# The second batch of a fused linear-attention and channel-mix kernel: loads and attention by halves of heads, later weights in another order

## Chip, cores and metric

The kernel runs on one core of a Trainium2 chip. The metric is the device time of one execution in microseconds (us); lower is better. Inputs are float32 in HBM (the chip's main memory), the output is float32, and the matrix work is done in bf16 with float32 sums in PSUM.

## The reference

Two stages, one after the other, on 8 batches of 576 tokens with 8 heads of 64 (so 512 channels):

```python
kv  = einsum('bhsd,bhse->bhde', k, v)              # 64 x 64 for each head: no softmax
out = einsum('bhsd,bhde->bhse', q, kv)
out = out / sqrt(mean(out * out, -1) + 1e-6) * g_norm       # by head
x   = out.transpose(0, 2, 1, 3).reshape(B, S, 512)
x_prev = x shifted by one token (zeros first)
xk = mu_k * x + (1 - mu_k) * x_prev                # likewise xr with mu_r
kk = maximum(xk @ w_k, 0)                          # 512 -> 1024
v  = (kk * kk) @ w_v                               # 1024 -> 512
y  = sigmoid(xr @ w_r) * v                         # 512 -> 512
```

## The kernel before

Nothing is scheduled by a compiler. One list of words, `ORDER`, is walked from its first word to its last, and each word emits its instructions. An engine executes its own instructions in the order in which they were emitted, so the list is the schedule of every engine. The list has eight strings, one about for each batch. A word reads like this: `Kp.0.1.2'=4` is the operation `Kp` with arguments 0, 1, 2; the mark `'` puts its evacuation (the copy out of PSUM) on VectorE instead of ScalarE; the digits after `=` name the PSUM banks (0 to 7) that it takes. A bank is given back by the operation that reads it last, so a word that takes a bank waits for that reader.

The work of one batch and the words for it:

- `ld` (line 188): loads k, v or q of a batch with a cast to bf16, issued on the GpSimd queue (POOL). The tiles for batches 1 to 7 have one buffer for each of k, v and q, so the load for the next batch waits for the last read of the present one. Batch 1 is loaded before the list begins, as are the weights, in the order w_k (two column halves), k, v, q, w_r, w_v (two row halves).
- `kv`, `kvo`: the 64 x 64 products of all heads and their copies; `qt`, `qto`: transposes of q for a half of the heads (M is 0 or 1) and their copies; `u`: q times kv, in three parts (token tiles 2 and 3; tiles 0 and 1; the odd first 64 tokens); `sq`, `red`, `nw`: squares on ScalarE, their sums on VectorE, and eight small VectorE steps for 1/rms by Newton's method; `mul`: times 1/rms; `x`, `x0` and `xo`, `x0o`: transposes back to channels by tokens, into `xT`.
- `dif`, `sc`, `fu`, `add`, `wrap`: differences of neighbouring tokens and the mixes `xk` and `xr`.
- `K`, `Kp` (line 485): xk times w_k with a Relu; `ks`, `ksp`: the squares, into `sqk`; `V` (line 521): a tile of 128 tokens of the product with w_v, in two parts of four matmuls; `R` (line 511): the product with w_r and the sigmoid; `fin` (line 534): their product and the store.

Batch 0 has its own path with words that end in c (`kvc`, `qtc`, `uc`, `sqc`, `msc`, `rsc`, `mcc`): its rms is a matmul with a matrix of 1/64 (`msc`) and ScalarE's Abs_reciprocal_sqrt (`rsc`). `Kp.0.0.n` are the eight pieces of batch 0 for tokens 256 to 575 ("high"), `Kp.0.1.n` the four for tokens 0 to 255 ("low"). `tab` loads ScalarE's table set with the sigmoid; the set with Abs_reciprocal_sqrt is loaded at the start. `wm.n` emits n matmuls of zeros whose result nobody reads. The last tile of the last batch is done by `L.0` and `L.1`, in two halves of the columns.

The prediction follows TensorE through the first of the eight strings, up to `Kp.1.0.0`, the first Relu product of batch 1, which opens the second.

Of the kernel before, what the change touches and what calls it, by code (L numbers as in the profile page):

```python
# [9 lines left out]
FP32 = mybir.dt.float32  # L10
# [9 lines left out]
    wm.2=1 cast.1' wm.4=2 cast.0 wm.1=3 kvc.0.2=45 kvco.0' kvco.1' qtc.0.2=67 qtco.0 qtco.1' uc.1=0 sqc.1 uc.0=1  # L20
    sqc.0 qtc.2.2=23 qtco.2' qtco.3' cols=4 msc.1=5 rsc.1 msc.0=7 rsc.0 mcc.0 mcc.1 difh.0.0.256.576 wm.2=6
    sc.0.0.1.256.576' kvc.2.1=2 kvco.2 uc.4=3 kvc.3.1=5 kvco.3 sc.0.0.0.256.576' uc.2=4 sqc.2 uc.3=6 sqc.3
    uc.5=7 sqc.5 msc.2=2 rsc.2 add.0.0.0.256.576 mcc.2 wm.4=1 msc.3=0 rsc.3 mcc.3 difh.0.1.256.576
    fu.0.0.2.256.576 sqc.4 msc.4=5 rsc.4 fu.0.0.3.256.576 Kp.0.0.0'=1 wrap.0 msc.5=2 rsc.5 mcc.5 mcc.4
    dif.0.0.256 fu.0.0.0.0.256 fu.0.0.1.0.256 sc.0.1.0' fu.0.0.3.0.256 fu.0.0.2.0.256 tab Kp.0.0.1=0 Kp.0.0.2=4
    Kp.0.0.3=6 Kp.0.0.4'=5 Kp.0.0.5=1 sc.0.1.1 sc.0.1.2 add.0.1.0 ksp.0.0.0.4 sc.0.1.3 add.0.1.1 Kp.0.0.6=2
    Kp.0.0.7'=7 Kp.0.1.0=3 Kp.0.1.1=0 Kp.0.1.2'=4 ksp.0.1.0.4 Kp.0.1.3=6 kv.1=15 kvo.1.0' ld.0.2 qt.1.0=23
    qto.1.0.0' qt.1.1=70 qto.1.1.0 qto.1.0.1' kvo.1.1 qto.1.1.1' u.1.0=41 sq.1.0.0 sq.1.0.1 red.1.5.9 u.1.2=6
    sq.1.2.0 u.1.1=23 sq.1.1.0 sq.1.1.1 red.1.0.5 nw.1.0.1 nw.1.1.2 nw.1.2.3 R.0.0=7 R.0.1=5 nw.1.3.4 R.0.2=0
    R.0.3=7 V.0.2.0=5 V.0.0.0=0 ksp.0.1.4.8 V.0.3.0=7 V.0.0.1 nw.1.4.5 nw.1.5.6 nw.1.6.7 ksp.0.0.4.8 nw.1.7.8  # L30
    mul.1.0.0 mul.1.0.1 x.1.2.2=41 xo.1.2.2.0 mul.1.1.0 V.0.2.1 xo.1.2.2.1 mul.1.1.1 x.1.0.2=23 mul.1.2.0
    x0.1=64 xo.1.0.2.1 x0o.1.1 fin.0.0 V.0.3.1 dif.1.384.576 xo.1.0.2.0' V.0.1.0=0 x0o.1.0' sc.1.0.2.384.576'
    sc.1.0.3.384.576' V.0.1.1 sc.1.0.0.384.576 sc.1.0.1.384.576 adda.1.0.384.576 wrap.1 dif.1.0.384
    sc.1.0.0.0.384' sc.1.0.1.0.384' sc.1.0.3.0.384 ld.1.2
    """,
    """
    Kp.1.0.0=1 Kp.1.0.1=3 Kp.1.0.2=2 sc.1.0.2.0.384' kv.2=46 kvo.2.0 kvo.2.1 ld.2.2 fin.0.1 add.1.0.1.0.384
    qt.2.1=10 sc.1.1.1' qto.2.1.0 add.1.0.0.0.384 ld.0.3 qt.2.0=32 qto.2.0.0' sc.1.1.3 sc.1.1.0' qto.2.0.1
    Kp.1.0.3=4 Kp.1.1.0=6 Kp.1.1.1=1 Kp.1.1.2=3 qto.2.1.1' u.2.0=02 add.1.1.0 u.2.2=4 sq.2.2.0 u.2.1=61 sq.2.1.1
    sq.2.1.0 fin.0.2 fin.0.3 sc.1.1.2' add.1.1.1 sq.2.0.1 sq.2.0.0 Kp.1.1.3'=5 R.1.4=7 ksp.1.1.0.2 red.2.0.5  # L40
    red.2.5.9 nw.2.0.1 nw.2.1.2 nw.2.2.3 ld.1.3 R.1.5=3 R.1.6=5 R.1.7=7 R.1.8=3 nw.2.3.4 nw.2.4.5 nw.2.5.6
    nw.2.6.7 nw.2.7.8 mul.2.1.0 Kp.1.1.4=5 mul.2.0.0 Kp.1.1.5=7 ksp.1.1.2.4' Kp.1.1.6=3 Kp.1.1.7=5 V.1.4.0=6
    mul.2.1.1 mul.2.2.0 ksp.1.1.4.6 ksp.1.1.6.8 kv.3=07 mul.2.0.1 x.2.0.4=31 xo.2.0.4.1' wrap.2 xo.2.0.4.0
# [73 lines left out]
def kernel(  # L117
# [13 lines left out]
    nc = tc.nc  # L131
# [121 lines left out]
    def half(i):  # L253
        return slice(64 * i, 64 * i + 64)
# [288 lines left out]
    for name in "kvq":  # L543
        load(name, 1)
# [99 lines left out]
```

## Time and profile before

| what | value |
|---|---|
| median of 3 runs | 204.22 us (204.13 to 204.47) |
| the profiled execution | 203.88 us, of which 202.1 us are the profile's span |
| TensorE (PE) busy | 192.2 us, 95% |
| VectorE (DVE) / ScalarE (ACT) busy | 161.8 us, 80% / 140.3 us, 69% |
| last matmul ends | 197.78 us |
| granted TensorE clock, mean | 0.995 |

The span is cut into stretches; "busy" is the time with at least one instruction on the engine, and an engine's idle time is put down to what released it. Matmuls are pipelined, so a row for 36 small matmuls can be longer than the time that passes until the next group starts.

### The profile page before, as it was taken

How to read it: one execution, taken by the hardware profiler on the slowest of the kernel's cores; microseconds unless marked ns; L12 is line 12 of the kernel's file. 1: busy time of each engine (PE TensorE's matmuls, PEld its weight loads, DVE VectorE, ACT ScalarE, POOL GpSimd, SP SyncE). 2: the span in 40 equal slices, each digit the busy share in tenths (PEclk: the TensorE clock that was granted, in tenths of full speed). 3: DMA queues.
4: the chain of work that ended last, by engine and by line, in shares of the span. 5: the costliest groups of instructions: out<-in, count | busy, mean ns of one | idle time of the engine just before them, and what ended most of it. 6: DMA issues, size and time to landing. Idle time of an engine off the chain costs nothing.

```text
span 202.1 us, 6329 instructions
## 1 busy us (share of the span) xinstructions
PE 192.2 (95%) x2684; PEld 116.4 (58%) x2684; DVE 161.8 (80%) x350; ACT 140.3 (69%) x273; POOL 24.1 (12%) x40
## 2 busy tenths in 40 slices
PE   7877889999999999999999999999999999999991
PEld 2534764485555568466565766576575455755450
DVE  1478859999979799998999999998898979974241
ACT  3476989579887888718897898977857474542420
POOL 7750040030021002202010004000000000000000
PEclk9999999999999999999999999999999999999998
DMA  6999999969959940998955604990001502226074
GB/s 208 217 206 207 208 209 205 209 143 175 246 83 218 224 130 0 157 224 208 203 79 104 159 2 63 206 284 15 5 0 29 131 0 55 67 48 145 3 190 123
DMA packets 21360, 27.22 MB, mean 135 GB/s; under 512 B 1740, under 2 KB 16340, under 8 KB 21332
## 3 DMA queue, kind: packets, MB, share of 16 engines
q0 software_dynamic: 14848, 16.19, 49.6%
q1 hardware_dynamic: 6164, 10.23, 18.4%
q10 hardware_dynamic: 320, 0.39, 0.7%
q8 instruction: 21, 0.34, 0.7%
q14 instruction: 7, 0.06, 0.1%
HBM read 33.56 MB, written 9.44 MB: 213 GB/s over the span
## 4 chain that ended last, share of the span: by engine, by line
PE 92%; DVE 4%; ACT 1%; issue 0%
PE ps_v L521 30%; PE ps_km L485 29%; PE ps_r L511 16%; PE ps_warm L245 4%; PE ps_u L307 3%; PE ps_qt L285 2%; PE ps_kv L271 2%; PE ps_x L363 2%; DVE xk L467 1%; DVE xT L440 1%; PE ps_v L529 1%; DVE qT L203 1%; PE ps_kv L400 1%; DVE dx L455 1%; ACT rs L436 1%; PE ps_ms L432 1%
## 5 line engine op out<-in xcount | busy, mean ns | idle before, releaser
L485 PE MATMUL ps_km<-xk,wk_sb 128*128 128x288 bf16 (+4 forms) x512 | 67.8, 286 | 1.5 <-DVE xk L467 1.5
L521 PE MATMUL ps_v<-wv_sb,sqk 128*128 128x512 bf16 x280 | 64.9, 379 | 0.0
L485 PEld LDWEIGHTS <-wk_sb 128*128 128x128 bf16 x512 | 49.2, 98 | 19.9 <-issue 1.7
L489 ACT ACTIVATE rt<-ps_km 128x288 bf16<-128x288 f32 (+3 forms) x87 | 36.0, 430 | 22.9 <-PE ps_km L485 20.2
L521 PEld LDWEIGHTS <-sqk 128*128 128x128 bf16 x280 | 26.7, 98 | 29.4
L511 PE MATMUL ps_r<-wr_sb,xr 128*128 128x512 bf16 x144 | 33.9, 379 | 0.0
L534 DVE TENSOR_TENSOR out_sb<-ps_v,sig 128x512 f32<-128x512 f32 (+1 forms) x37 | 23.9, 669 | 11.1 <-ACT sig L514 8.6
L514 ACT ACTIVATE sig<-ps_r 128x512 bf16<-128x512 f32 x36 | 21.3, 603 | 13.0 <-PE ps_r L511 9.3
L495 ACT ACTIVATE sqk<-rt 128x576 bf16<-128x576 bf16 (+4 forms) x32 | 24.2, 781 | 0.1
L461 ACT ACTIVATE m<-dx,cols 128x576 bf16<-128x576 bf16 (+2 forms) x27 | 18.7, 741 | 5.5 <-DVE dx L455 5.5
L511 PEld LDWEIGHTS <-xr 128*128 128x128 bf16 x144 | 13.7, 98 | 15.0 <-DVE xr L478 0.3
L316 DVE TENSOR_REDUCE ss<-sq 128x16 f32<-128x1024 bf16 (+1 forms) x14 | 18.7, 1347 | 3.1 <-ACT sq L312 2.9
L348 DVE TENSOR_TENSOR y<-ps_u,rs 128x512 bf16<-128x512 f32 (+1 forms) x35 | 20.0, 628 | 0.3
L312 ACT ACTIVATE sq<-ps_u 128x512 bf16<-128x512 f32 (+1 forms) x35 | 16.6, 562 | 2.7 <-PE ps_u L307 2.5
L491 DVE TENSOR_SCALAR rt<-ps_km 128x288 bf16<-128x288 f32 (+3 forms) x33 | 14.6, 463 | 1.7 <-PE ps_km L485 1.5
L188 POOL DMA_DIRECT2D in_k<-in_k_dram x7 | 5.2, 743 | 85.6 <-PE ps_kv L271 74.2
L201 ACT COPY qT<-ps_qt 128x576 bf16<-128x576 bf16 x20 | 12.4, 636 | 4.0 <-PE ps_qt L409 2.7
L478 DVE TENSOR_TENSOR xr<-m,xT 128x1152 bf16<-128x1152 bf16 x16 | 12.0, 752 | 1.8 <-ACT m L461 1.5
L463 DVE TENSOR_SCALAR m<-dx,cols 128x576 bf16<-128x576 bf16 (+3 forms) x39 | 12.6, 356 | 0.2
L478 DVE TENSOR_TENSOR xk<-m,xT 128x1152 bf16<-128x1152 bf16 (+2 forms) x16 | 11.1, 698 | 1.4 <-ACT m L461 1.2
L455 DVE TENSOR_TENSOR dx<-xT 128x2304 bf16<-128x2304 bf16 (+4 forms) x11 | 11.3, 1031 | 0.7
L497 DVE TENSOR_TENSOR sqk<-rt 128x576 bf16<-128x576 bf16 (+1 forms) x25 | 11.1, 453 | 0.7 <-ACT rt L489 0.7
(63 smaller groups left out, 143.5 us busy)
## 6 DMA issues: line engine op xcount, KB each, us to landing
out_dram<-out_sb SPq DMA_DIRECT2D x68, 128.0 KB, 3.4
in_k<-in_k_dram POOLq DMA_DIRECT2D x7, 576.0 KB, 6.4
in_v<-in_v_dram POOLq DMA_DIRECT2D x7, 576.0 KB, 10.1
in_q<-in_q_dram POOLq DMA_DIRECT2D x7, 576.0 KB, 12.8
wk_sb<-in_moe_w_k_dram POOLq DMA_DIRECT2D x2, 512.0 KB, 10.3
wv_sb<-in_moe_w_v_dram POOLq DMA_DIRECT2D x2, 512.0 KB, 20.8
sqk<-in_k_dram SPq DMA_DIRECT2D x1, 576.0 KB, 3.8
q<-in_q_dram POOLq DMA_DIRECT2D x2, 288.0 KB, 6.6
```

The lines of the kernel that those rows point to most:

```text
L312: ACT.activation(out=sq[:, rg(t0, n, i) if n else slice(0, 1)], in_=held["u", a, part, i][1], func=AF.Square)
L316: DVE.tensor_reduce(out=ss[:, g0:g1], in_=sq[:, g0:g1], op=ALU.add, axis=AX.X)
L348: DVE.tensor_mul(out=y[:, g], in0=give(("u", a, part, i)), in1=rs[:, g].unsqueeze(3).to_broadcast([128, max(n, 1), NHP, HD]))
L461: eng.activation(out=out_, in_=in_, func=AF.Copy, scale=mu)
L478: DVE.tensor_add(out=dst, in0=m[:, hs, c0:c1], in1=x[:, hs, c0:c1])
L485: nc.tensor.matmul(ps[:, n, :], wk_sb[:, cc, 128 * fc:128 * fc + 128], at[b]["xk"][:, cc, c0:c1], start=(cc == 0), stop=(cc == NHP - 1))
L489: eng.activation(out=dst, in_=ps, func=AF.Relu)
L495: eng.activation(out=sqk[:, fcs, o:o + n], in_=src, func=AF.Square)
L511: nc.tensor.matmul(ps, xr[:, cc, 128 * t:128 * t + 128], wr_sb[:, cc, :], start=(cc == 0), stop=(cc == NHP - 1))
L514: ACT.activation(out=sig[b, t], in_=give("r"), func=AF.Sigmoid)
L521: nc.tensor.matmul(ps, sqk[:, fc, 128 * t:128 * t + 128], wv_sb[:, fc, :], start=(fc == 0), stop=(fc == NFC - 1))
L534: DVE.tensor_mul(out=o, in0=give(key), in1=sig[b, t][:, c])
```

## The change

The second batch (batch 1) gets operations for a half of its heads, M = 0 or 1: `kvh`, `kvho`, `uh`, `sqh`, `redh`, `rsh`, `mulh`, `x0h`, `x0ho`, `xh`, `xho`. They do what the words without h do, on two of the four head pairs. Its 1/rms is `rsh`, Abs_reciprocal_sqrt on ScalarE, in place of the eight Newton steps. Its loads are six halves, and w_v is loaded as one half and two quarters: the order after w_k is k, q, v of the first half, w_v's first half, k, q, v of the second half, w_v's two last quarters, w_r. `Vq` is `V` with two matmuls for each part; batch 0's four tiles in the first string use it. `ORDER` is written anew in all its eight strings; the first is shown, and from the last its end.

```diff
@@ ORDER, first string @@
-    wm.2=1 cast.1' wm.4=2 cast.0 wm.1=3 kvc.0.2=45 kvco.0' kvco.1' qtc.0.2=67 qtco.0 qtco.1' uc.1=0 sqc.1 uc.0=1
-    sqc.0 qtc.2.2=23 qtco.2' qtco.3' cols=4 msc.1=5 rsc.1 msc.0=7 rsc.0 mcc.0 mcc.1 difh.0.0.256.576 wm.2=6
-    sc.0.0.1.256.576' kvc.2.1=2 kvco.2 uc.4=3 kvc.3.1=5 kvco.3 sc.0.0.0.256.576' uc.2=4 sqc.2 uc.3=6 sqc.3
-    uc.5=7 sqc.5 msc.2=2 rsc.2 add.0.0.0.256.576 mcc.2 wm.4=1 msc.3=0 rsc.3 mcc.3 difh.0.1.256.576
-    fu.0.0.2.256.576 sqc.4 msc.4=5 rsc.4 fu.0.0.3.256.576 Kp.0.0.0'=1 wrap.0 msc.5=2 rsc.5 mcc.5 mcc.4
...
+    wm.4=1 wm.4=2 cast.1' cast.0 kvc.0.2=34 qtc.0.2=56 qtco.0' kvco.0' uc.0=7 qtco.1 kvco.1 uc.1=0 sqc.0 msc.0=1
+    qtc.2.2=25 qtco.2' sqc.1 msc.1=3 rsc.0 cols=6 mcc.0 qtco.3' kvc.2.1=4 rsc.1 kvco.2 uc.2=1 mcc.1
+    difh.0.0.256.576 sc.0.0.1.256.576' kvc.3.1=2 kvco.3 sqc.2 uc.5=6 uc.3=3 msc.2=4 sqc.3 msc.3=7 rsc.2
+    sc.0.0.0.256.576' rsc.3 sqc.5 add.0.0.0.256.576 uc.4=5 msc.5=2 sqc.4 msc.4=0 rsc.4 wm.2=4 rsc.5 mcc.2 mcc.3
+    wm.2=7 difh.0.1.256.576 wrap.0 fu.0.0.2.256.576 fu.0.0.3.256.576 mcc.4 Kp.0.0.0=1 Kp.0.0.1=3 mcc.5
+    dif.0.0.256 sc.0.1.1 sc.0.1.3 fu.0.0.0.0.256 fu.0.0.2.0.256 Kp.0.0.2=4 Kp.0.0.3'=0 Kp.0.0.4=7 sc.0.1.0
+    fu.0.0.1.0.256 fu.0.0.3.0.256 Kp.0.0.5=2 Kp.0.0.6'=5 Kp.0.0.7'=1 Kp.0.1.0=6 ksp.0.0.0.4 qt.1.0=30 qto.1.0.0'
+    sc.0.1.2' qto.1.0.1' kvh.0=47 kvho.0.0' kvho.0.1 Kp.0.1.1=5 add.0.1.1 uh.0.0=12 uh.1.0=63 sqh.1.0.0
+    sqh.1.1.0 uh.2.0=0 sqh.2.0.0 ksp.0.0.4.8' ksp.0.1.0.4' redh.0.5.0 sqh.0.1.0 sqh.0.0.0 Kp.0.1.2=4 Kp.0.1.3=7
+    Vq.0.3.0=5 Vq.0.3.1 rsh.0.5.0 redh.5.9.0 mulh.2.0.0 Vq.0.2.0=4 Vq.0.2.1 rsh.5.9.0 x0h.0=70 ksp.0.1.4.8
+    mulh.0.0.0 mulh.0.1.0 xh.2.2.0=12 mulh.1.0.0 xho.2.2.0.0 mulh.1.1.0 x0ho.0.1' x0ho.0.0 qt.1.1=63 qto.1.1.0
+    xh.0.2.0=10 xho.2.2.0.1' kvh.1=72 qto.1.1.1' kvho.1.1 kvho.1.0' uh.1.1=36 xho.0.2.0.0 uh.0.1=72 xho.0.2.0.1'
+    uh.2.1=0 sqh.1.1.1 sqh.2.0.1 sqh.1.0.1 redh.0.5.1 Vq.0.1.0=1 Vq.0.1.1 Vq.0.1.2 Vq.0.2.2 sqh.0.1.1 sqh.0.0.1
+    redh.5.9.1 rsh.0.5.1 mulh.1.1.1 rsh.5.9.1 Vq.0.3.2 Vq.0.3.3 mulh.2.0.1 Vq.0.0.0=6 Vq.0.0.1 mulh.0.0.1 ld.0.2
+    Vq.0.0.2 mulh.1.0.1 xh.0.2.1=07 mulh.0.1.1 xh.2.2.1=32 Vq.0.2.3 add.0.1.0 xho.2.2.1.1' tab Vq.0.1.3
+    xho.0.2.1.1' xho.2.2.1.0 dif.1.384.576 sc.1.0.0.384.576' sc.1.0.2.384.576 ld.1.2 sc.1.0.3.384.576' x0h.1=23
+    wrap.1 x0ho.1.1' x0ho.1.0 xho.0.2.1.0 R.0.0=7 R.0.1=2 dif.1.0.384 sc.1.0.1.0.384' sc.1.0.3.0.384
+    sc.1.0.2.0.384' R.0.2=3 sc.1.0.1.384.576' adda.1.0.384.576 R.0.3=0 sc.1.1.0 Vq.0.0.3 fin.0.0 sc.1.0.0.0.384
+    sc.1.1.1
...
@@ ORDER, end of the last string @@
-    fin.6.3 R.7.6=5 fin.7.4 R.7.7=4 V.7.6.1 fin.7.5 V.7.7.0=3 V.7.7.1 fin.7.6 fin.7.7 R.7.8=1 L.0=7 L.1=0
+    V.7.5.0=6 V.7.5.1 R.7.5=7 R.7.6=3 R.7.7=4 fin.6.3 fin.7.4 fin.7.5 fin.7.6 V.7.7.0=0 V.7.7.1 R.7.8=2 fin.7.7
+    L.0=5 L.1=7 wm.1=6
@@ loads ahead of the list @@
-    load_w(wk_sb, moe_w_k, cols_=2)
-    for name in "kvq":
-        load(name, 1)
-    load_w(wr_sb, moe_w_r)
-    load_w(wv_sb, moe_w_v, rows_=2)
+    for what in "wk.0.2 wk.1.2 k.0.2 q.0.2 v.0.2 wv.0.2 k.1.2 q.1.2 v.1.2 wv.2.4 wv.3.4 wr.0.1".split():
+        name, i, n = what.split(".")
+        (load_x if name in dram else load_w)(name, int(i), int(n))
     warm(12)
@@ new functions (some of them) @@
+    def load_x(name, i, n):
+        if i == 0:
+            x_in[name, 1] = inp.tile([128, NHP, GX], BF16, tag=f"in_{name}", name=f"in_{name}")
+        ms = slice(NHP // n * i, NHP // n * (i + 1))
+        nc.gpsimd.dma_start(out=x_in[name, 1][:, ms], in_=by_token(dram[name], 1)[:, ms])
+    def square_h(part, i, M):
+        sq, (t0, n) = mine(1, "sq", [128, NRG, NHP, HD], BF16), TILES[part]
+        ACT.activation(out=sq[:, rg(t0, n, i) if n else slice(0, 1), pair(M)], in_=held["uh", part, M, i][1],
+                       func=AF.Square)
+    def reduce_h(g0, g1, M):
+        sq, ss = at[1]["sq"], mine(1, "ss", [128, NRG, NHP], FP32)
+        DVE.tensor_reduce(out=ss[:, g0:g1, pair(M)], in_=sq[:, g0:g1, pair(M)], op=ALU.add, axis=AX.X)
+    def root_h(g0, g1, M):
+        ss, y = at[1]["ss"], mine(1, "rs", [128, NRG, NHP], FP32)
+        ACT.activation(out=y[:, g0:g1, pair(M)], in_=ss[:, g0:g1, pair(M)], func=AF.Abs_reciprocal_sqrt,
+                       scale=1.0 / HD, bias=eps)
+    def mult_h(part, i, M):
+        y, rs, (t0, n) = mine(1, "y", [128, NRG, NHP, HD], BF16), at[1]["rs"], TILES[part]
+        g = rg(t0, n, i) if n else slice(0, 1)
+        DVE.tensor_mul(out=y[:, g, pair(M)], in0=give(("uh", part, M, i)),
+                       in1=rs[:, g, pair(M)].unsqueeze(3).to_broadcast([128, max(n, 1), 2, HD]))
...
-    def vv(b, t, part):
+    def vv(b, t, part, n=4):
...
-        for fc in range(4 * part, 4 * part + 4):
+        for fc in range(n * part, n * part + n):
```

## The prediction, as it was written before the run

> **What bounds the kernel now.** I read the page's slices first: where is TensorE not full?
>
> ```profile
> PE   7877889999999999999999999999999999999991
> ACT  3476989579887888718897898977857474542420
> DMA  6999999969959940998955604990001502226074
> ```
>
> TensorE (PE) is full from the seventh slice (30 us) to the last; what can be won lies before it and in the last slice. The waits of PE say what it missed:
>
> ```profile
> PE ps_km L485 <- DVE xk L467: 1.5, 3, 0.8
> PE ps_warm L245 <- DVE eps L208: 1.2, 1, 1.2
> PE ps_ms L432 <- ACT sq L426: 1.0, 1, 1.0
> PE ps_u L307 <- DVE qT L203: 0.7, 2, 0.5
> PE ps_u L421 <- DVE qT L203: 0.6, 1, 0.6
> PE ps_u L421 <- ACT kv L201: 0.5, 2, 0.2
> ```
>
> Without the start that is 4.3 us; none waits for a DMA. The timeline of PE places the late ones:
>
> ```profile
> 22.47 3.44 PE L485 MATMUL ps_km<-xk,wk_sb 128*128 128x256 bf16 x30 [0.54 <-DVE xk L467]
> 25.84 0.78 PE L271 MATMUL ps_kv<-in_v,in_k 64*64 64x64 bf16 x72
> 26.43 0.89 PE L285 MATMUL ps_qt<-ident,in_q 64*64 64x64 bf16 x72
> 27.53 0.20 PE L307 MATMUL ps_u<-kv,qT 64*128 64x64 bf16 x2 [0.21 <-DVE qT L203]
> 28.23 0.96 PE L307 MATMUL ps_u<-kv,qT 64*128 64x64 bf16 x38 [0.49 <-DVE qT L203]
> ...
> 40.44 0.74 PE L485 MATMUL ps_km<-xk,wk_sb 128*128 128x192 bf16 x7
> ```
>
> The last row is Kp.1.0.0. Up to it both kernels do the same TensorE work: the same matmuls, and 25 of zeros, one of them now after L.1. So the question is when PE gets there. From 22.47 it takes 17.97 us, 0.70 of it waits. Batch 1's loads:
>
> ```profile
> 7.83 0.74 POOL L188 DMA_DIRECT2D in_k<-in_k_dram  x1 [0.42 <-DMA q<-in_q_dram]
> 9.32 0.74 POOL L188 DMA_DIRECT2D in_v<-in_v_dram  x1 [0.75 <-DMA q<-in_q_dram]
> 10.05 0.75 POOL L188 DMA_DIRECT2D in_q<-in_q_dram  x1
> ...
> DMA to landing us min/median/max: 12.8/14.6/16.2
> ```
>
> They land at 20.6, 23.9 and 26.3; w_r (issued 10.8, 18.1 to landing) at 28.9, w_v's halves (11.5 and 12.3; 19.9 and 21.7) at 31.4 and 34.0, w_k's second half (6.5; 11.2) at 17.8. They come one after the other. The first two rows' waits end with two landings of batch 0's q, halves of 0.29 MB, 1.5 us apart.
>
> **The loads.** From 17.8 to 26.3 three wholes, so 1.42 us for a half. After: k, q, v of half 0 at 19.2, 20.6, 22.0; w_v's half 24.6; half 1 at 26.0, 27.5, 28.9; w_v's quarters 30.2 and 31.4; w_r 34.0. POOL issues four DMAs more, but always stands behind several undrained ones. Batch 2's loads wait for half 1's last reads, at 30 instead of 27 us, but queue behind w_r in both: 36.8 and 39.8 for k and v, read at about 41. The walk below reads the weights one and a half to two us after they land (w_v's half at 26.6, its quarters at 32.0 and 33.3, w_r at 36.4), so none of this is on the path.
>
> **Batch 0, walked from rows.** Twenty zero matmuls stand ahead of the first kv instead of nineteen: 0.86 us for four, so +0.22. If they are no cover for anything else, that is a plain loss. Then VectorE copies qT (0.45) before kv (0.22), which was hidden before: the first u +0.13 more. Six zero matmuls in the middle become four, on no path. High part: rsc.2 and rsc.3 come level with before (14.4, 14.9); VectorE's row of difh 0.49, two sc 0.52, add 0.49, two mcc 1.14, difh 0.49, wrap 0.22, two fu 1.02 ends at 17.4 instead of 17.41: no change. Low part: msc.4 and msc.5 no longer stand behind Kp.0.0.0 on PE, so the last rsc ends at 17.3, not 18.53, and dif.0.0.256 starts at 18.5, not 19.74. Now PE itself is last: 29 of the high matmuls after 17.4 by 0.136 end at 21.35, xk's last piece 21.3. Low starts at 21.35 instead of 22.47: **-1.12**.
>
> **Batch 1, half 0.** PE: Kp.0.1.0 (8 by 0.109) to 22.2, qt and kvh (36 each, 0.41 and 0.36) to 23.0, Kp.0.1.1 to 23.85; loads are there. But the copy kvho.0.1 stands on ScalarE behind Kp.0.1.0's Relu (0.61, from 22.4) and ksp.0.0.0.4 (1.27): it ends at 24.4, and uh waits: **+0.50**. Behind that wait PE holds all else. Next: squares (128x256: row 0.388) to 26.4 on ScalarE, the sums on VectorE, which until 26.1 makes ksp. No row has a sum over 640 or 512; those of 1280 and 1024 (1.48, 1.21) on a line give 0.81 and 0.67; bounds 0.67 and 1.21. The second ends at 27.4. rsh (128x20 and less) has no row either: bounds are the cast of 64 (0.21) and the rs of 384 (0.58); I take 0.25, nearest in size. 27.75; two mulh (0.41 each, overlapping by 0.1) free xh at 28.6. PE's cover is Kp.0.1.2 and .3 (1.74), eight quarter-piece matmuls (1.73), x0h: until 28.43. Waits **+0.16**, then qt.1.1's banks 6 and 3, which mulh.1.x give back at 29.2: **+0.38**.
>
> **Half 1.** qt to 29.6, xh, kvh to 30.15; then uh needs ScalarE's copy of qT (0.64) and kv (0.27), 30.7: **+0.53**, small ones 0.05. From 31.2 twelve V matmuls (2.6) cover the chain to mulh.1.1.1, which frees bank 6 at 33.8, with nothing to spare. (The copy xho of 256 lies between the rows of 128 and 512, 0.36 and 0.68; 0.47 on the line, the ends move x0h.1 by 0.1 or 0.2, which the V ahead of it covers.) R.0.1 takes bank 2 from x0ho.1.0, on ScalarE behind a scale of batch 1 that waits for VectorE's difference (36.8 + 0.45 + 0.36): **+0.30**. The Newton steps (8 by 0.23 on VectorE, 1.9 us) go; they were covered. Sum of waits 1.92 instead of 0.70: +1.22. With -1.12, Kp.1.0.0 starts **0.10 later** than 40.44.
>
> **A price for the table load.** It moves from 18.55, where it took 1.28 and the next ScalarE instruction followed at 19.84, to about 33.6, before xho.2.2.1.0, which waits for PE until 35.6: free by that row. The Trainium skill, "ScalarE: Activation LUTs", section "What ACT_TABLE_LOAD costs", adds a drain of about 1.38 us to each switch; by it the sum would be +0.6, and the trace does not show that drain.
>
> **Behind the stage.** In the second string uh's whole-batch counterpart u.2 waits for its two qT copies (0.64 each, ScalarE) and VectorE's two fin of batch 0: **+0.15**. PE ends Kp.1.1.1 at 46.25, the copies at 46.4. In the later strings, written anew, no row shows a wait to be priced; I count nothing there and leave what they may hold to the upper end. At the end R.7.8's sigmoid is now emitted before fin.7.7, whose store blocked ScalarE until 196.8; L.0's store leaves earlier, and L.1's, issued at 198.46 behind it (its multiply ended at 198.23), can go 0.2 earlier: **-0.19**. The zero matmul behind L.1 runs beside the store.
>
> Sum: 0.10 + 0.15 - 0.19 = +0.06 on the profiled execution (203.88 = span 202.1 + 1.78), so 203.94; the median stood 0.34 above it: **204.3**.
>
> **Rivals.** (1) *Slower: the sums and roots by halves are dear.* If a half's sum costs 1.21 and rsh 0.58, each half's chain grows by 0.40 + 0.33; in both halves nothing covers it (0.16 late in the first, no slack in the second): +1.46, so 205.7. It decides once the second sum of half 0 ends after 27.4. For: fixed costs (256 elements 0.39, 512 elements 0.61). Against: small VectorE steps of 36 take 0.2. Chance 0.30. (2) *Faster: the short chain is hidden.* If squares and multiplies of 256 cost half the whole (0.28 for 0.39, 0.31 for 0.41) and the sum 0.61, the waits 0.16 and 0.38 go, half 1 wins 0.2, and R.0.1's 0.30 goes with an earlier xT: -1.0, so 203.2. For: equal steps follow each other closer than their lengths (three of 0.49 within 1.42). Against: the 0.39 row. Chance 0.33. (3) *Halved loads cost as much as whole ones.* Then v's half 0 lands at 26.3, kvh waits 3.7 us for it, of which 0.5 replaces the copy's wait: 207.5. Against: q's halves. The Trainium skill, "DMA: Bandwidth & Descriptors", section "Anatomy of one DMA — SWDGE (gpsimd) path", has such a rule: about 2.0 us fixed for each DMA. The landings 1.5 us apart speak against it where DMAs queue. Chance 0.03. (4) *The table load waits for ScalarE to empty.* If that costs as much again as its own row, 1.28, ScalarE is busy from 33.6 to 36.2, and xho.2.2.1.0, x0ho.1.0 and R.0.1 come 0.6 later: 204.9. Against: the row of 18.55 has the next instruction right behind it. The Trainium skill's drain, named above, is this rule. Chance 0.04.
>
> **The numbers.** 0.2%, 0.41 us, is about what a measurement can tell here (the runs of before spread over 0.17%). The forecast (within 0.2%) has 0.30, rivals 0.30, 0.33, 0.03, 0.04. Faster 0.33; same 0.30; slower 0.37. The forecast's own range is 203.9 to 204.7. The whole range takes in (2) with 0.2 to spare and (1) and (4) with 0.3 for the later strings: 203.0 to 206.0; half-load costs (3) stay out.
>
> **What the profile after would show.** Right: low Kp (128x256) at about 21.4; the first uh waiting half a microsecond for ScalarE's kv; Kp.1.0.0 (128x192) at 40.5; PE without waits behind 47; the last store issued some 0.2 us closer to the last multiply. Wrong: a wait of PE for a DMA; low Kp after 22; a root over 0.4; waits of over 2.5 us in sum between 24 and 38, or under 1; any PE wait in the later strings.

## The result, and the profile after

| | before | after |
|---|---|---|
| median, first comparison | 204.34 us (4 runs) | 206.35 us (4 runs: 205.87, 206.52, 208.54, 206.18) |
| ratio, 95% interval | | 1.0114 [1.0066, 1.0162] |
| profiled execution / its span | 203.88 / 202.1 us | 205.87 / 204.1 us |
| granted TensorE clock, mean | 0.995 | 0.992 |

Slower, by 1.0% in the medians; the forecast was 204.3 and its range ended at 206.0. The ratio is the time after over the time before. Runs over 1.5% above the fastest of their kernel are left out of the ratios here and below. The page's slices of the kernel after:

```profile
PE   7869999999989999999999999999999999999992
PEclk9996999999999999999999999999999999999999
ACT  3385898699896988488895999997938338385140
DMA  6999999999969912796697439900045101381364
```

TensorE is full three slices earlier than before (from the fourth, 15 us, except for the twelfth), which looks like a gain. The second row says why this profile has none from it: in the fourth slice TensorE had a lower granted clock; in the kernel before this row holds nines up to its last slice. A busy engine at half clock is full too. The same stage cut at the moments where the clock record changes (columns: window, its length, busy time of PE and matmuls, granted clock, DMA share, GB/s):

```profile
12.97:16.38 3.41, 2.07 (x14) 1.00 1.24 204
16.38:19.79 3.41, 3.41 (x13) 0.50 1.22 208
19.79:23.20 3.41, 3.41 (x27) 1.00 1.21 203
```

For 3.41 us the clock is 0.50: 13 matmuls start there, 27 in the next window of the same length. PE's timeline of the kernel after:

```profile
1.20 6.92 PE L259 MATMUL ps_warm<-zeros 128*128 128x512 bf16 x20 [1.20 <-DVE eps L222]
8.04 0.48 PE L414 MATMUL ps_kv<-rt 64*64 64x64 bf16 x36
...
16.12 1.64 PE L259 MATMUL ps_warm<-zeros 128*128 128x512 bf16 x4
17.55 6.49 PE L567 MATMUL ps_km<-xk,wk_sb 128*128 128x320 bf16 x40
...
42.20 0.82 PE L567 MATMUL ps_km<-xk,wk_sb 128*128 128x192 bf16 x8
...
57.72 0.70 PE L377 MATMUL ps_x<-ident,y 64*128 64x64 bf16 x36
59.14 0.80 PE L299 MATMUL ps_qt<-ident,in_q 64*64 64x64 bf16 x72 [0.72 <-DMA in_q<-in_q_dram]
```

The four zero matmuls in the middle stand at 16.12, at the end of the thin window, and two of them and the first high Kp lie in the half-clock window; the low Kp start at 23.00. In the kernel before, the six middle zeros and the window that held the last four are these:

```profile
10.48 0.59 PE L245 MATMUL ps_warm<-zeros 128*128 128x512 bf16 x2
13.37 1.03 PE L245 MATMUL ps_warm<-zeros 128*128 128x512 bf16 x4
12.45:15.87 3.42, 2.14 (x16) 1.00 1.23 202
```

The last row of the kernel after's timeline is qt.3 of the second string: it stands ahead of V.1.5, V.1.4 and V.1.6 now, and q of batch 3 lands at 59.1. In the kernel before those V tiles (24 matmuls) came first and q, at 57.95, had long landed:

```profile
57.52 5.36 PE L521 MATMUL ps_v<-wv_sb,sqk 128*128 128x512 bf16 x24
62.81 0.78 PE L285 MATMUL ps_qt<-ident,in_q 64*64 64x64 bf16 x72
```

The difference of the two profiled executions, from starts of matmuls, beside what the prediction's terms give for each part:

| part | before | after | difference | predicted |
|---|---|---|---|---|
| start of the first kv | 7.57 | 8.04 | +0.47 | +0.22 |
| from there to Kp.1.0.0 | 32.87 | 34.16 | +1.29 | -0.12 |
| from there to the last V matmul (L.1) | 157.05 | 157.62 | +0.57 | +0.15 |
| from there to the end of the span | 4.58 | 4.27 | -0.31 | -0.19 |
| sum | 202.07 | 204.09 | +2.02 | +0.06 |

The half clock is not the whole loss: of the four runs above, those of 206.18 and 206.52 had a granted clock of 1.0. Neither left a trace; a later execution of the same kernel, 206.44 at full clock, did (below).

### The profile page after: what moved, and what is told of

Same layout as the page of the kernel before. It is cut to its first block, busy times and chain, and to the rows that moved or that the text cites. A ratio compares the mean times of both kernels' runs of the same rounds, so it can differ in the third digit from the quotient of the medians.

```text
span 204.1 us, 6336 instructions
## 1 busy us (share of the span) xinstructions
PE 195.2 (96%) x2684; PEld 117.3 (57%) x2684; DVE 159.0 (78%) x340; ACT 145.6 (71%) x299; POOL 26.8 (13%) x44
## 3 DMA queue, kind: packets, MB, share of 16 engines
q1 hardware_dynamic: 6164, 10.23, 19.2%
## 4 chain that ended last, share of the span: by engine, by line
PE 88%; DMA 6%; ACT 2%; DVE 1%; issue 0%
PE ps_v L603 29%; PE ps_km L567 29%; PE ps_r L593 13%; DMA in_q<-in_q_dram 6%; PE ps_warm L259 4%; PE ps_qt L299 3%; PE ps_u L321 2%; PE ps_x L377 2%; PE ps_kv L285 2%; PE ps_v L611 1%; ACT sq L440 1%; DVE y L502 1%; ACT rs L450 1%; PE ps_u L482 1%; PE ps_u L435 1%
## 5 line engine op out<-in xcount | busy, mean ns | idle before, releaser
L571 ACT ACTIVATE rt<-ps_km 128x288 bf16<-128x288 f32 (+3 forms) x92 | 38.4, 431 | 16.2 <-PE ps_km L567 10.3
L616 DVE TENSOR_TENSOR out_sb<-ps_v,sig 128x512 f32<-128x512 f32 (+1 forms) x37 | 24.4, 670 | 13.4 <-ACT sig L596 5.4
L577 ACT ACTIVATE sqk<-rt 128x576 bf16<-128x576 bf16 (+4 forms) x38 | 27.1, 740 | 0.2
L543 ACT ACTIVATE m<-dx,cols 128x576 bf16<-128x576 bf16 (+2 forms) x31 | 22.5, 753 | 3.5 <-DVE dx L537 3.4
L573 DVE TENSOR_SCALAR rt<-ps_km 128x288 bf16<-128x288 f32 (+2 forms) x28 | 12.8, 465 | 7.4 <-PE ps_km L567 6.5
L326 ACT ACTIVATE sq<-ps_u 128x512 bf16<-128x512 f32 (+1 forms) x30 | 14.7, 567 | 3.9 <-PE ps_u L321 3.9
L362 DVE TENSOR_TENSOR y<-ps_u,rs 128x512 bf16<-128x512 f32 (+1 forms) x30 | 17.3, 629 | 0.2
L330 DVE TENSOR_REDUCE ss<-sq 128x16 f32<-128x1024 bf16 (+1 forms) x12 | 16.0, 1346 | 1.3 <-ACT sq L326 1.2
L215 ACT COPY qT<-ps_qt 128x576 bf16<-128x576 bf16 x15 | 9.4, 648 | 4.8 <-PE ps_qt L423 3.1
L217 DVE COPY qT<-ps_qt 128x576 bf16<-128x576 bf16 x17 | 7.6, 451 | 5.4 <-PE ps_qt L423 3.5
L545 DVE TENSOR_SCALAR m<-dx,cols 128x576 bf16<-128x576 bf16 (+3 forms) x35 | 11.6, 356 | 0.3
L369 DVE TENSOR_SCALAR xT<-ps_x,cols 128x1024 bf16<-128x1024 bf16 (+3 forms) x22 | 10.2, 478 | 1.7 <-PE ps_x L377 1.6
## 6 DMA issues: line engine op xcount, KB each, us to landing
in_q<-in_q_dram POOLq DMA_DIRECT2D x6, 576.0 KB, 11.9
```

What stands on the lines that cost most here:

```text
L326: ACT.activation(out=sq[:, rg(t0, n, i) if n else slice(0, 1)], in_=held["u", a, part, i][1], func=AF.Square)
L330: DVE.tensor_reduce(out=ss[:, g0:g1], in_=sq[:, g0:g1], op=ALU.add, axis=AX.X)
L362: DVE.tensor_mul(out=y[:, g], in0=give(("u", a, part, i)), in1=rs[:, g].unsqueeze(3).to_broadcast([128, max(n, 1), NHP, HD]))
L543: eng.activation(out=out_, in_=in_, func=AF.Copy, scale=mu)
L571: eng.activation(out=dst, in_=ps, func=AF.Relu)
L573: eng.tensor_scalar(out=dst, in0=ps, scalar1=0.0, scalar2=None, op0=ALU.max)
```

## The experiments

The `-`/`+` lines below are words of `ORDER`, cut to the words that change; `...` stands for words left out. A "half-clock stretch", or stretch for short, is a time at a granted clock of one half, and a "half-clock run" is a run whose mean granted clock is under 0.994: one stretch of 3.41 us at half clock takes 0.008 of it; half clock in the last microseconds, as before's profile has from 200.19 on, takes up to 0.005 and does not count. The kernel before ran beside each group of kernels, and the groups ran on several chips; over these groups it has 204.16 us in the median of 84 runs without a stretch and 206.5 in that of 26 half-clock runs. "Release" is the moment at which the trace's clock record goes to full speed during the head's zeros.

### The middle zeros, and q ahead

**Middle zeros earlier.** Edit of the kernel after:

```diff
-    uc.4=5 msc.5=2 ... rsc.4 wm.2=4 rsc.5 mcc.2 mcc.3 wm.2=7 difh.0.1.256.576
+    uc.4=5 wm.4=0 msc.5=2 ... rsc.4 rsc.5 mcc.2 mcc.3 difh.0.1.256.576
```

> The changed kernel, with its four zero matmuls in the middle moved from behind msc.4 (PE at 16.1 us) to behind uc.4 (14.6 us), into a gap in which PE waits 0.77 us for a square; nothing else. Clock theory: the changed kernel's profile has the granted clock at one half from 16.4 to 19.8 us, because the zeros no longer stand in the stretch before it. Then the half-clock stretch goes here, the high Relu products of 320 columns come 0.136 us apart instead of 0.267 from the start, the low ones (256) begin at 21.7 instead of 23.0, and the time falls by 1.3 us. Rival (the half clock is an accident of one execution, and the waits by halves of heads cost the two microseconds): no gain over 0.3 us.

Measured: 204.81 us, ratio to before 1.0036 [1.0006, 1.0066]; one half-clock run of 10. In the profile the clock is 1.0, low Kp start at 21.23, Kp.1.0.0 at 40.42, and q's wait of 0.8 is still there. Kp.1.0.0 stands 32.82 us behind the first kv instead of 34.16, the 1.3 us of the clock theory. The median gains less, 0.5 against the kernel after beside it (205.29, below), because only three of that kernel's ten runs had a stretch there.

**The kernel before without its six middle zeros.**

```diff
-    difh.0.0.256.576 wm.2=6 ... mcc.2 wm.4=1 msc.3=0
+    difh.0.0.256.576 ... mcc.2 msc.3=0
```

> The kernel before without its six zero matmuls in the middle (two behind the first msc, four behind msc.2); the nineteen at the start stay. Clock theory: the clock is cut to one half for some 3.4 us between 12 and 23 us here too, and the kernel is slower by 1 to 1.5 us. Rival (accident): same time within 0.3 us, or faster by what the zeros take on the path (up to 0.3), at full clock.

Measured: 205.36 us, 1.0035 [1.0001, 1.0070]; ten half-clock runs of ten. Windows of its profile, cut as above:

```profile
11.26:14.68 3.42, 2.24 (x47) 1.00 1.25 208
14.68:18.09 3.41, 1.79 (x6) 0.50 1.23 207
18.09:21.50 3.41, 3.41 (x15) 0.50 1.21 208
```

Work that nobody reads, taken out, makes the kernel before 1.1 us slower in the median, with a stretch in every run, where the kernel before beside it had one in six runs of 27: those zeros held the clock. Both stretches begin at a whole number of windows behind the release: 4.43 + 3 x 3.413 = 14.67 here, 6.14 + 3 x 3.413 = 16.38 in the kernel after. The Trainium skill, "TensorE: Matmul & The Clock Gate", section "What's actually happening", calls the activity window free-running and 3413 ns long, so that a kernel meets it at another phase in each execution; these two traces agree, with 3.41 us and releases at 4.43 and 6.14. The Trainium skill's rule against idle gaps over some 3.4 us (section "HAM oscillation — how this bites in real kernels") is not enough here: in the window that cost the kernel after its clock, 12.97 to 16.38, two matmuls start at most 1.0 us apart.

**q loaded ahead.** Two buffers for q; batch 2's q loaded behind w_r:

```diff
-    mulh.0.0.1 ld.0.2 ... Kp.1.0.3=7 ld.2.2
+    mulh.0.0.1 ld.2.2 ld.0.2 ... Kp.1.0.3=7
```

> The changed kernel with two buffers for q, and the load of batch 2's q emitted ahead of batch 2's k and v, so that it queues right behind w_r. In the changed kernel the DMAs ran dry at 31 to 34 us (batch 2's k was issued at 32.4), and qt.3 waited 0.9 us for batch 3's q, which landed at 59.1. Load theory: the dry stretch is filled, batch 3's q lands before 58.3, the wait at 58.3 goes or falls under 0.3, kv.2 still finds its v (by 42.5), and the time falls by 0.6 to 0.9. Rival (the wait has another cause, the squares of batch 1 that V.1.5 needs at 59.2, or the loads only change places and kv.2 or kv.3 wait instead): under 0.3.

Measured: 205.85 us (seven runs, one of them 286.29), 1.0071 [1.0047, 1.0096]: no gain, as the rival has it. PE waits 1.3 us for q, and 0.8 for v, where the profile of the kernel after had no wait for v. That the loads changed places is not shown by this, because two later executions of the unedited kernel have the same two waits. What is shown is that loading q ahead is not the cure.

**The kernel after, again.** No edit.

> The changed kernel once more, for a second profile. Clock theory: half clock again for about 3.4 us before 23 us, at a place that may be up to a window away, and 206.0 to 206.5 us. Rival (accident): no half-clock stretch in the profile, and the time near 205.

Measured: 205.29 us, 1.0046 [1.0014, 1.0077], three half-clock runs of ten. Its profile is the fastest run of that kernel, 203.57 us: release at 3.85, no stretch, Kp.1.0.0 at 39.93. The clock theory expected a stretch in this profile and missed; the stretch comes in some executions only.

### The head, q of batch 3, the halves of the loads

**Fewer head zeros**, on top of the earlier middle zeros (12 more are emitted ahead of the first string):

```diff
-    wm.4=1 wm.4=2 cast.1' cast.0
+    wm.1=1 wm.1=2 cast.1' cast.0
```

> The changed kernel with its four middle zero matmuls earlier (as in the run before with zeros earlier) and 14 zero matmuls at the head instead of 20. Theory A (the head's zeros run at half clock, 0.427 us each, until the clock is granted, and in the traces so far it was granted anywhere between 3.85 and 7.22 us; the 20 zeros therefore end, and the first kv matmul starts, between 6.91 and 8.58 us, and since the changed kernel has no wait for a load in its first string, that delay reaches the end): the first kv starts at 6.8 to 7.2 whenever the clock comes, Kp.1.0.0 up to 0.8 earlier than 40.42, the median 0.4 to 0.8 us below that kernel's 204.81, and the upper end of its runs (206.2) comes down by about 1 us. Theory B (the head's zeros cover the wait for the casts anyway, and a thinner head delays the granted clock): no gain, or a half clock in the profile before 25 us and a time 1 us above.

Measured: 203.75 us, 0.9981 [0.9955, 1.0007]; no half-clock run in ten. That is 1.06 below the kernel with the earlier zeros alone, more than theory A had. In the profile the first kv starts at 6.70 and Kp.1.0.0 at 39.99, but PE waits 1.3 us for batch 3's q: TensorE comes earlier, and in this execution the load does not (57.52, against 57.41 with the old head). In the profile of a later kernel with this head it landed at 56.54, and the wait was 0.4.

**qt.3 behind V.1.5 and V.1.4**, with the earlier middle zeros and the old head:

```diff
-    qt.3.0=67 ... qt.3.1=32 qto.3.1.1 qto.3.1.0 V.1.5.0=1 V.1.5.1 V.1.4.0=4 V.1.4.1
+    V.1.5.0=1 V.1.5.1 V.1.4.0=4 V.1.4.1 qt.3.0=67 ... qt.3.1=32 qto.3.1.1 qto.3.1.0     (ksp.1.1.2.4 behind ksp.1.1.6.8)
```

> The changed kernel with its four middle zeros earlier, and in the second string qt.3 (both halves and their copies) behind V.1.5 and V.1.4 instead of ahead of them, with ksp.1.1.2.4, which V.1.5 reads, emitted on ScalarE before the multiplies of batch 2. Theory A (TensorE stands idle 0.8 us there, because q of batch 3 lands 0.8 us after its place in the order, and the idle time is pure loss): no PE wait for a DMA in the trace, the last matmul 0.8 us earlier, median about 204.0 against 204.81. Theory B (the wait only moves: V.1.5 waits for its squares or u.3 waits for the later copies of qT): some 0.3 to 0.8 us of new PE waits between 56 and 66 us, and a median within 0.3 of 204.8.

Measured: 205.15 us, 1.0033 [1.0014, 1.0053]; the five runs without a stretch have 204.79 in the median, against 204.61 for the nine of the kernel with the earlier zeros alone. PE no longer waits for q, but a K tile of the third string waits for its bank:

```profile
69.85 2.37 PE L567 MATMUL ps_km<-xk,wk_sb 128*128 128x288 bf16 x18 [0.50 <-ACT rt L571]
```

The wait moved, as theory B has it, but further on than B had it. Five half-clock runs of ten show as well that the earlier zeros alone do not settle the clock: in this profile the window that lost it is 8.07 to 11.49 (PE busy 2.16 us), ahead of the place of the four zeros, where PE waits 0.5 us for batch 0's q.

**Whole loads for batch 1**, with the earlier middle zeros:

```diff
-    k.0.2 q.0.2 v.0.2 wv.0.2 k.1.2 q.1.2 v.1.2 wv.2.4 wv.3.4 wr.0.1
+    k.0.1 q.0.1 v.0.1 wv.0.2 wv.2.4 wv.3.4 wr.0.1
```

> The changed kernel with its four middle zeros earlier and batch 1's k, q, v loaded whole (k, q, v, then w_v's half, its quarters, w_r), the attention by halves kept. Theory A (the halved loads carry the change): v lands at about 26.1 instead of 21.9, kvh.0, at 22.55 with halved loads, waits some 3.5 us for it, half 1's wait of 0.33 goes, Kp.1.0.0 comes at 43.5 to 44.0 instead of 40.42 and the median at 207.8 to 208.3. Theory B (the order of the halves on TensorE has enough other work ahead): under 1 us lost, under 205.8.

Measured: 210.18 us (four runs, each with a stretch), 1.0258 [1.0185, 1.0330].

```profile
23.80 0.48 PE L299 MATMUL ps_qt<-ident,in_q 64*64 64x64 bf16 x36 [1.07 <-DMA in_q<-in_q_dram]
26.28 0.48 PE L464 MATMUL ps_kv<-in_v,in_k 64*64 64x64 bf16 x36 [2.01 <-DMA in_v<-in_v_dram]
```

v lands at 26.14 and kvh.0 starts at 26.28 instead of the 22.55 of the profile with the earlier zeros alone. Kp.1.0.0 comes 4.96 later than there; 0.46 of that is the later head, some 1.3 a half-clock window (26.66 to 30.08), which follows on the 3.1 us of waiting, the rest, 3.2, the loads. Theory A had the wait right and the time 2 us too low, for want of the stretch. The halves of the loads carry the change.

**The kernel before with fewer head zeros** (13 instead of 19):

```diff
-    wm.2=1 cast.1' wm.4=2 cast.0 wm.1=3 kvc.0.2=45
+    wm.1=1 cast.1' cast.0 kvc.0.2=45
```

> The kernel before with 13 zero matmuls at the head instead of 19. Theory A (there the load of batch 1's q, landing at 26.3, stands just ahead of its transposes at 26.4, so that a head that is earlier wins nothing and only a late head shows): the first kv at 6.8 to 7.0, a PE wait for q's or v's landing of 0.3 to 0.6 between 24 and 27 us, median 204.0 to 204.3 against 204.25. Theory B (the head's delay reaches the end in the kernel before as well): median 203.5 to 203.8. Theory C (a thinner head costs the clock): a half clock in the profile and 205 or more.

Measured: 204.7 us, 0.9996 [0.9959, 1.0032]; six half-clock runs of ten, and 203.97 in the median of the other four. The first kv starts 0.72 earlier than in before's profile, Kp.1.0.0 only 0.04 earlier. Theory A's time came, to 0.03, in the runs without a stretch, but not its reason: no PE wait between 24 and 27 us names a load. The first high Kp is already only 0.05 earlier; ahead of it PE waits 0.3 for batch 0's last v (11.9 us). C's half clock came in the other six runs (204.64 to 205.47), though not in the profile; the kernel before beside it had six of 25.

### Together, and each alone

**Combined**: earlier middle zeros, fewer head zeros, and

```diff
-    qtco.0' kvco.0' uc.0=7 qtco.1 kvco.1 ... qt.3.0=67 ... V.1.5.0=1 V.1.5.1     (ksp.1.1.2.4 ahead of ksp.1.0.0.8)
+    kvco.0' qtco.0' uc.0=7 kvco.1 qtco.1 ... V.1.5.0=1 V.1.5.1 qt.3.0=67 ...     (ksp.1.1.2.4 behind ksp.1.1.6.8)
```

> The changed kernel with its four middle zeros earlier, 14 head zeros instead of 20, the copies of batch 0's kv ahead of those of qT on both engines, ksp.1.1.2.4 emitted before the multiplies of batch 2, and V.1.5 (eight matmuls, 1.73 us) ahead of qt.3. Theory A (q of batch 3 lands at 57.5 whatever TensorE does, and 1.73 us of work ahead of it fills the 1.5 us that the thinner head left idle there, while the later copies of qT still come before u.3): no PE wait for a DMA, the time from Kp.1.0.0 to the last matmul 1.0 to 1.5 us shorter than with the thinner head alone, median 202.4 to 203.0. Theory B (as with qt.3 behind two V tiles, the wait moves to a K tile's bank in the third string): 203.4 to 203.9.

Measured: 203.26 us, 0.9965 [0.9948, 0.9982]: faster than both kernels. Two half-clock runs of 12. PE's row for qt.3:

```profile
56.47 1.90 PE L603 MATMUL ps_v<-wv_sb,sqk 128*128 128x512 bf16 x8
58.30 0.80 PE L299 MATMUL ps_qt<-ident,in_q 64*64 64x64 bf16 x72
```

q lands at 57.0, and eight V matmuls cover it. From Kp.1.0.0 to the start of the last V matmul it takes 157.12 us, 1.15 less than in the profile with the earlier zeros and fewer head zeros: the mechanism of A, but the median is 0.26 above its range. The 1.15 is too high as a price for qt.3's place, because that profile had the late q; the run without the new place of qt.3, below, gives 0.45.

**Fewer head zeros alone** (the head's edit above on the kernel after, its middle zeros in their places).

> The changed kernel with 14 zeros at the head instead of 20, and nothing else. Theory A (the head's delay and the half clock in the middle are two separate losses): its median 0.8 to 1.1 below the changed kernel in the same call, some 204.3 to 204.8, with a half clock (mean clock 0.993 or less) still in a third of its runs. Theory B (the head's zeros hold the clock for the middle): a half clock in most runs, and no gain.

Measured: 205.34 us, 1.0018 [0.9976, 1.0060]: 1.06 below the kernel after beside it, as A has it; but eight half-clock runs of 12, as B has it. The four others lie at 203.52 to 203.72. So the head is a loss of its own: without a stretch it is 203.6 against 204.9. That a thinner head makes the clock's loss more likely is not shown here, since the kernel after beside it had seven of 12.

**The kernel after, a third time.**

> The changed kernel as it is, as the measure for the other runs of this call: 205.3 to 206.4, a mean clock of 0.993 or less in a third of its runs; in the profile the first kv at the time that the release of the clock gives (1.2 us, then 0.427 us for each zero up to the release and 0.216 after it), and Kp.1.0.0 32.5 to 33.0 us behind it, 1.4 more if a half clock comes between.

Measured: 206.4 us, 1.0062 [1.0025, 1.0099]; seven half-clock runs of 12. The profile: release at 3.96, first kv at 7.16 (0.2 late), and batch 0's last v lands at 13.34 instead of 11.6 to 11.9:

```profile
13.48 0.47 PE L414 MATMUL ps_kv<-rt 64*64 64x64 bf16 x18 [1.69 <-DMA rt<-in_v_dram]
```

PE is busy for only 1.25 us of the window around this wait (10.79 to 14.20), and two windows at half clock follow (14.20 to 21.02). Kp.1.0.0 stands 36.59 behind the first kv, where I expected 32.5 to 33.0, plus 1.4 with a stretch: a late load and the clock add up.

**Head, earlier zeros, and kv copied first** (the combination without its edit of qt.3).

> The changed kernel with middle zeros earlier, 14 head zeros, and batch 0's kv copied ahead of its qT as in the kernel before. Theory A (the first u waits 0.69 us for VectorE's kv, which stands behind the copy of qT): the first u starts 0.10 to 0.15 earlier behind the first kv matmul (1.70 instead of 1.82 us), median 0.1 below the 203.75 of the run without the swap. Theory B (the wait passes to the copy of qT, and the later steps wait for the loads of heads 2 and 3): first u earlier, median unchanged.

Measured: 204.05 us, 1.0001 [0.9973, 1.0028]; five half-clock runs of 12. The first u starts 1.74 behind the first kv instead of 1.82, a little less than A had; the median of the seven runs without a stretch, 203.66, is that of the ten without the swap, 203.75, within their spread. A gain of the swap is not shown; the runs without it are from another chip. Against this kernel, on the same chip, the combination's runs without a stretch (203.21) are 0.45 faster: that is qt.3's place.

### Why executions differ, and whether the filling decides

Four more executions of the kernel after, without an edit:

> The changed kernel as it is, one execution more with its trace. Theory A (an execution's time is settled by the release of the clock, by half-clock stretches of 3.41 us that follow from it, and by a late landing of batch 0's last loads): with the release at r us, the first kv matmul starts at r + (20 - (r - 1.2)/0.427) x 0.216 + 0.08 (7.60 for r = 5.25, 8.58 for 7.22); Kp.1.0.0 follows 32.8 to 33.1 us behind it, plus 1.3 to 1.7 for each half-clock stretch before it and plus what a load of batch 0 lands later than 11.8; the span ends 161.8 to 162.1 us behind Kp.1.0.0. Theory B (something later in the kernel varies as well): the last stretch differs from that by over 0.4, or the first by over 0.4 with none of these causes.

> The changed kernel as it is, another execution with its trace; the same two theories and the same numbers as in the look before.

> The changed kernel as it is, a third execution with its trace; the same two theories and the same numbers.

> The changed kernel as it is, a fourth execution with its trace; the same two theories and the same numbers.

| execution | time | release | first kv, by the formula | first kv, measured | to Kp.1.0.0 | half clock before it | from there to the end |
|---|---|---|---|---|---|---|---|
| 1 | 206.44 | 6.88 | 8.41 | 8.41 | 32.83 | no | 163.42 |
| 2 | 204.85 | 6.70 | 8.32 | 8.32 | 32.83 | no | 161.93 |
| 3 | 208.34 | 5.37 | 7.66 | 7.66 | 34.15 | 15.61 to 19.02 | 164.75 |
| 4 | 205.97 | 6.06 | 8.00 | 8.00 | 34.15 | 16.30 to 19.72 | 162.05 |

Up to Kp.1.0.0 theory A holds: the first kv comes to the hundredth where the formula puts it, and the way from there lies in A's range. The formula is for 20 zeros; with 14 the first kv waits for its operand as well (6.70 in the first such profile, where the formula has 6.37).

Why the second execution kept its clock and the third lost it, with the same instructions, is a matter of where the windows fall. Windows of the second, then of the third, cut as above:

```profile
13.53:16.94 3.41, 2.29 (x15) 1.00 1.24 206
12.19:15.60 3.41, 2.07 (x34) 1.00 1.23 204
15.60:19.02 3.42, 3.42 (x11) 0.50 1.22 207
```

In the second the four middle zeros start at 16.38 to 17.03, three of them before the thin window ends; in the third they start at 15.83, behind its end.

Behind Kp.1.0.0 theory B holds in the first and the third, by 1.3 us and more beyond A's range. PE in the first:

```profile
56.96 0.77 PE L285 MATMUL ps_kv<-in_v,in_k 64*64 64x64 bf16 x72 [0.70 <-ACT sig L596]
57.66 0.70 PE L377 MATMUL ps_x<-ident,y 64*128 64x64 bf16 x36
59.70 0.80 PE L299 MATMUL ps_qt<-ident,in_q 64*64 64x64 bf16 x72 [1.34 <-DMA in_q<-in_q_dram]
```

In the first, a run of 206.44 at full clock, batch 3's v and q land at 56.83 and 59.66; in the second, whose loads were issued at the same times within 0.3 us, at 55.29 and 58.06. The row of 56.96 names ScalarE's sigmoid, but it starts right behind v's landing. In the third the clock was lost once more, from 59.98 to 63.39, behind such waits. Why the loads landed later in two of four executions is not settled by these traces and stays open.

**Filled waits.** Three single zeros at batch 0's waits, once on the combined version, and once, with four zeros behind uc.4 and its own four left, on the kernel after:

```diff
-    kvco.2 uc.2=1 ... kvc.3.1=2 ... sqc.3 msc.3=7     (kernel after only: ... uc.4=5 msc.5=2)
+    kvco.2 wm.1=6 uc.2=1 ... wm.1=6 kvc.3.1=2 ... sqc.3 wm.1=5 msc.3=7     (... uc.4=5 wm.4=0 msc.5=2)
```

> The combined version with three single zero matmuls more, each where TensorE waits in batch 0 anyway: ahead of uc.2, of kvc.3.1 and of msc.3 (waits of 0.31, 0.27 and 0.30 us there, a zero takes 0.216). Theory A (a half-clock stretch follows when a window of 3.41 us between 8 and 18 us holds too little work, and a filler in the waits cures it at no cost): no run with a mean clock under 0.994, where the combined version had 2 of 12, median 203.1 to 203.4, the highest run under 203.9. Theory B (the stretches come from something else than the filling): as often as before, a sixth or more of the runs.

> The changed kernel with the same three single zeros, and four more behind uc.4, its own four in the middle left in their places; the head and the second string untouched. Theory A: no half-clock stretch in 12 runs, where the changed kernel had one in 14 of 30; the median falls from 206.2 to that of its full-clock runs, 205.0, or up to 0.2 above for zeros that no wait hides; the runs still spread from 203.7 to 206.5, by the release and by batch 3's loads. Theory B: half-clock stretches in a third or more of the runs, median 205.8 or more.

Measured: the combination 203.24 us (203.12 to 203.85), no half-clock run in 12, 0.9930 [0.9895, 0.9964] to before, which had eight of 23 beside it; against before's runs without a stretch, 204.20, it is 0.9953. The kernel after: 205.28 us, 1.0027 [0.9985, 1.0068], two half-clock runs of 12, the others from 204.24 to 206.18. That lies between the two theories, and the median is that of the kernel after on the same chip (205.29), so a faster median is not shown. Half-clock runs by how full batch 0's waits are:

| kernels | half-clock runs |
|---|---|
| before without its middle zeros | 10 of 10 |
| middle zeros late (the kernel after, q ahead, the head alone) | 14 of 30, 5 of 7, 8 of 12 |
| middle zeros earlier (five kernels with the halved loads) | 13 of 54 |
| the waits filled (two kernels) | 2 of 24 |
| the kernel before | 26 of 110 |
| the kernel before with 13 head zeros | 6 of 10 |

The place of the zeros decides how often, if not to the last run: late against earlier or filled is 8 of 17 against 3 of 34 on the chip that ran the filled kernels, and 17 of 28 against 7 of 24 on another. What the single zeros add to the earlier ones is not shown: two of 24 stand against one of ten for the earlier zeros alone on that chip. A threshold can't be read off PE's busy time: the windows of 2.07, 2.16 and 2.24 us cost the clock; 2.14 (before, 12.45 to 15.87) and 2.29 (the first two of the four executions) did not.

## Why the prediction was wrong, step by step

- **"Six zero matmuls in the middle become four, on no path."** This is the step that failed. The count hardly matters; their place does. Before they stood at 10.5 and 13.4 us, inside the thin windows; after, at 16.1, at their end or behind it. Nobody waits for a zero matmul, so the walk along releasers finds no price for it; its price is 1.3 us for a single stretch, and 14 of the kernel's 30 runs are half-clock runs. The prediction has no term for the granted clock.
- **"Twenty zero matmuls stand ahead of the first kv instead of nineteen ... +0.22."** The term was mis-sized: it priced the zeros at 0.216. Up to the release they take 0.427, and the release came between 3.85 and 7.22 us, so the first kv starts between 6.91 and 8.58; at the same release one zero more does cost 0.22, and in the two profiles it was +0.47 because the release came 0.51 later. From a first kv at 7.6 on, the delay reaches Kp.1.0.0 one to one (7.60 gives 40.42 in the profile with the earlier zeros, 8.32 gives 41.15 in the second of the four executions). "If they are no cover for anything else" was the right question: six fewer win 1.06 in the median, with the middle zeros late (206.40 to 205.34, whose intervals overlap) and earlier (204.81 to 203.75, on different chips). "The first u +0.13 more" came as +0.04.
- **The low part: "Low starts at 21.35 instead of 22.47: -1.12".** The start is right without a stretch: 21.23 from a first kv at 7.60, where the walk had 7.79; 23.00 in the profiled run, 1.3 of it the clock. The difference is misread. The row at 22.47 holds 30 of the 32 low matmuls; in the kernel before two of them start at 21.56 already, ahead of the wait, in a row that bears the form of its first matmul:

```profile
21.42 0.52 PE L485 MATMUL ps_km<-xk,wk_sb 128*128 128x320 bf16 x3
```

For the same work the gain forecast was 0.90, not 1.12.
- **From low Kp to Kp.1.0.0.** Predicted 40.54 - 21.35 = 19.19 us; measured 42.20 - 23.00 = 19.20. Its parts were less exact: start-to-start waits of 1.47 us instead of 1.92 (uh 0.33 for +0.50, xh 0.13 for +0.16, qt.1.1 0.51 for +0.38, half 1's uh 0.49 for +0.53, R.0.1 none for +0.30). The 0.45 too much was offset: 0.22 by the two low matmuls of the misread row, the rest by work that the walk had at nothing and that is not broken down here. That the two agree to 0.01 is luck.
- **The short operations.** Two sums in 1.40 us, roots of 0.30, squares of 256 one every 0.28: the estimates held, and rival (1) fell, though its 205.7 lies nearest to the result, by luck. Rival (2) fell too: squares are short, but the waits stayed.
- **The loads.** Half 0 landed at 19.07, 20.47 and 21.88, for 19.2, 20.6 and 22.0: rival (3) fell, and the whole loads show what it would have cost. Rival (4): the table load took 1.28 us again, and ScalarE, idle 0.69 behind it, waited for PE.
- **"In the later strings ... no row shows a wait to be priced; I count nothing there."** Wrong: qt.3 stands 0.9 us (start to start) ahead of q's landing, and 1.5 with v's 0.9 on top where batch 3's loads land late. The row was there to price it: q's landing at 57.95 in the profile before, beside the new place of qt.3. u.2's +0.15 did not come.
- **The end.** L.1 to the end of the span: -0.31, predicted -0.19.

Of the signs of "wrong", three were seen: low Kp after 22, and, in one wait, a PE wait for a DMA and a PE wait in the later strings.

Over all runs: without a stretch the kernel after has 205.0 us in the median of 16 runs, 0.84 above before; with one, 206.9 in 14. Over all 30 it has 206.2, over before's 204.3: of 1.9 us some 1.0 is the clock (1.2 in the kernel after, less 0.1 that before loses by it). The rest, by the experiments above, is the head and the place of qt.3, and the 206.44 at full clock shows both: a first kv at 8.41, and batch 3's loads 1.5 us later than in the execution after it. With these three mended, the same change is faster than before: 0.9965 and 0.9930, with the intervals above, for the two combined versions.

## What to carry to other kernels

Look where the zero (or any idle-filling) matmuls stand before calling them free: read the granted clock's row window by window, and ask of each thin window what is left in it when they move. Do it for several executions, because the windows fall at another place in each. A kernel whose stage has lost its waits passes on the delays ahead of it; so price the head not from one execution, but from the spread of the release. And wherever an order is written anew, set each transfer's landing beside the place of its reader in the new order, in the later stages as well.

## What was not expected of the hardware

- Zero matmuls of 512 columns start 0.427 us apart until the clock's release and 0.216 after it. The release varied from 3.85 to 7.22 us between executions; later stretches begin and end at whole multiples of 3.41 us behind it, and one alone cost 1.3 us in this stage.
- A window of 3.41 us in which PE was busy for 2.07, never idle for 0.8 us at a time, cost the clock of the next; that window began 4.9 us behind the first kv. In another execution of the same kernel it began 5.2 us behind it, PE was busy for 2.29 us of it, and the clock stayed.
- Loads issued at nearly the same times (within 0.3 us) landed 1.5 us apart in two executions, with the queue in use by loads and stores.
